# Key sums and attention products with 64 stationary columns, in steps of eight heads

## The chip, the cores and the metric

The kernel runs on one core of a Trainium2 chip. The time is the device time of one execution in microseconds; for the kernel before, three runs were timed. A profile of one execution shows when each engine worked: PE (TensorE: matmuls, with PEld the loads of the stationary operand), DVE (VectorE), ACT (ScalarE), POOL (GpSimd) and SP, which issues the transfers.

## The reference

Linear attention with random features, followed by a feed-forward block with a residual. Batch 8, 8 heads, 576 positions, head size 64, 128 features, model width 512, hidden width 2048, everything fp32:

```python
def phi(x):
    proj = np.einsum('bhsd,md->bhsm', x, omega)
    h = proj - np.sum(x * x, axis=-1, keepdims=True) / 2.0
    return np.exp(h - np.max(h, axis=-1, keepdims=True)) / np.sqrt(m)
q_p, k_p = phi(q * scale), phi(k * scale)
kv = np.einsum('bhsm,bhsd->bhmd', k_p, v)
z = np.sum(k_p, axis=2)
num = np.einsum('bhsm,bhmd->bhsd', q_p, kv)
den = np.einsum('bhsm,bhm->bhs', q_p, z)[..., None] + 1e-06
x = num / den                      # (b, h, s, d), then to (b, s, h*d)
xn = (x - mean(x)) / sqrt(var(x) + 1e-06) * g_ln
out = x + np.maximum(xn @ w_ch1, 0.0) @ w_ch2
```

## The kernel before

**Work and tiles.** The 8 x 576 = 4608 positions are nine MLP tiles of 512 (t) or 36 chunks of 128 (c). A batch has four and a half chunks: for the keys, each batch has four whole chunks, and the two halves that are left of a pair of batches share one mixed chunk; among the query chunks, four of the 36 lie in two batches.

- *Keys* (`gen_k`): the projection (L510, line numbers as in the profile) fills two PSUM banks, DVE takes the maximum (L442), ACT the exponential (L448). Then the **key sums** (`sums`, L480): per head, the 128 positions by 128 features of `kp` are the stationary operand, and the values with a column of ones (65 columns) are the moving one. That gives `kv` and `z` together. From batch 1 on each chunk's result goes to a bank of its own, and `keep` (L495) adds it into `kv` in SBUF.
- *Queries* (`gen_q2`, `features`): a projection in two matmuls (L582, L583), the maximum over features on POOL, subtraction on DVE, the exponential on ACT.
- *Products* (`gen_x`, L671): per head, 128 features by 128 positions are the stationary operand, `kv` with its 65 columns the moving one. DVE divides (L678, L680, L682) and frees the bank. Mean and variance (L698, L700) and the root (`gen_rs`) follow, then the normalising (L741), four transposes on PE (L755), a copy on ACT (L759) and a subtraction on DVE (L761), which leave the normalised input in two fp32r parts.
- *MLP* (`mm1`, `mm2`): three matmuls for each product of tiles, from the high and low parts (L782 to L784, L815 to L817), moving 512 columns each. The hidden parts come from ACT (L793) and DVE (L795).

An fp32 matmul of a row of the program is two matmuls in the profile; those of the MLP are one.

**PSUM.** Of eight banks, once the MLP has begun, four hold its output, two its hidden products, and two (`b_at`) are for all of attention: projections, key sums, products and transposes.

**What sets the order.** `Plan` writes the whole program's order ahead of time, by a list of estimated costs: a part asks for a place (`get`), waits for a result (`wait`) or takes an engine for an estimated time (`us`, `act`, `dve`), and among the parts that could start first the one with the lowest rank is taken. The MLP has the last rank (`Plan.FILL`), so it fills what the others leave of PE. Each engine then runs its instructions strictly in that order. Before the MLP begins (`mlp_on` is empty) `warm` fills PE with bf16 matmuls (L308) that compute nothing.

In the kernel before, the key sums and the products are parts of four heads each, and each takes one bank of `b_at` (for a mixed chunk of keys: two, one for each batch). Four heads are given 0.9 us of PE.

Of the kernel before, what the change touches and what calls it, by code (L numbers as in the profile page):

```python
# [190 lines left out]
def favor_ffn(ctx, tc, kT, kTr, vF, vR, qT, qD, omT, gT, w1, w2, out):  # L191
# [30 lines left out]
    def us(eng, t):  # L222
        return "run", {eng: t}
# [16 lines left out]
    def wait(*key):  # L240
        return "wait", key
# [13 lines left out]
    def bank(tag, n=512):  # L255
        return tile_of(tag, [P, 512], F32, ps)[:, 0:n]
# [12 lines left out]
    def at_now():  # L269
        return b_at if mlp_on else banks  # L270
# [67 lines left out]
    def gen_w(n, f):  # L338
# [81 lines left out]
    def gen_k(b, c, kraw, v, early, t_v, n_kp):  # L420
        rank = plan.cur.rank
        yield dma(2 * P * NP * P)
        nc.sync.dma_start(kraw, kT[b, c] if c < NFULL else kTr[b // 2])
        nc.sync.dma_start(v, vF[b, c] if c < NFULL else vR[b // 2])
        if c:
            yield wait("k", b, c - 1)
        t_kp = yield "get", n_kp
        t_mb = yield "get", n_mb
        late = t_kp, t_mb, t_v
        done(("k", b, c))  # L430
        kp = tile_of(late[0], [P, H, M])
        mb = tile_of(late[1], [P, H])
        yield wait("om")

        def values():
            yield us(DVE, 0.08)
            nc.vector.memset(v[:, :, D : D + 1], 1.0)
            done(("v", b, c))

        def side(s, t_b, pk):  # L440
            yield dve(4 * M)
            nc.vector.tensor_reduce(  # L442
                out=mb[:, 4 * s : 4 * s + 4], in_=pk, axis=AX.X, op=ALU.max, negate=True
            )
            yield act(M, 4, 0.142)
            for i in range(4):
                j = 4 * s + i
                nc.scalar.activation(  # L448
                    out=kp[:, j], in_=pk[:, i], func=AF.Exp, scale=1.0, bias=mb[:, j : j + 1]
                )  # L450
            free(t_b)
            done(("kp", b, c, s))

        def sums(s):
            yield wait("v", b, c)
            yield wait("kp", b, c, 0)
            yield wait("kp", b, c, 1)
            if c:
                yield wait("kvmm", b, c - 1, s)

            parts = [(b, slice(0, P))] if c < NFULL else [(b, slice(0, REM)), (b + 1, slice(REM, P))]
            t_b = []
            for n, _ in parts:
                if n or c == 0:
                    t_b.append((yield "get", at_now()))
                else:
                    t_b.append(pvs[s])
            if b == c == 0:
                pvs[s] = t_b[0]
                pvt[s] = bank(t_b[0])  # L470
            pv = [
                (bank(x) if n else pvt[s])[:, 0 : 4 * (D + 1)].rearrange("p (a b) -> p a b", b=D + 1)
                for x, (n, _) in zip(t_b, parts)
            ]
            yield us(PE, 0.9 if b else 1.13)
            for i in range(4):
                h = 4 * s + i
                for o, (n, r) in zip(pv, parts):

                    nc.tensor.matmul(  # L480
                        o[:, i], kp[r, slot(h)], v[r, h],
                        start=(n > 0 or c + i == 0), stop=(n > 0 or (c == NFULL and i == 3)),
                    )
                warm(i % 2)
            done(("kvmm", b, c, s))
            for x, o, (n, _) in zip(t_b, pv, parts):
                if n or c == NFULL:
                    plan.add(rank, keep(n, s, x, o))

        def keep(n, s, t_b, pv):  # L490
            o = kvs[n][1][:, 4 * s : 4 * s + 4]
            if n and (c if n == b else 0) or (n % 2 and c < NFULL):
                yield wait(*kv_key(n, c - 1), s)
                yield dve(4 * (D + 1))
                nc.vector.tensor_tensor(out=o, in0=pv, in1=o, op=ALU.add)  # L495
# [153 lines left out]
    def gen_x(c, t_st, st):  # L649
        blk, cols = c // 2, (c % 2) * P  # L650
        ends = sorted({0, P, *(b * S - c * P for b in range(B) if 0 < b * S - c * P < P)})
        parts = [(a, z, (c * P + a) // S) for a, z in zip(ends, ends[1:])]
        for j in range(2):
            for s in range(2):
                yield wait("phi", blk, j, s)
# [5 lines left out]
        o = 16 * (c % 2)  # L661
        rank = plan.cur.rank

        def half(s):
            t_b = yield "get", at_now()
            yield us(PE, 0.9 * len(parts) if mlp_on else 1.13)
            pn = bank(t_b)[:, 0 : 4 * (D + 1)].rearrange("p (a b) -> p a b", b=D + 1)
            for i in range(4):
                h = 4 * s + i
                for a, z, b in parts:  # L670
                    nc.tensor.matmul(  # L671
                        pn[a:z, i], phi(blk, h, slice(cols + a, cols + z)), kvs[b][1][:, h], start=True, stop=True
                    )
                warm(i % 2)
            done(("nummm", c, s))
            dn = st[:, o + 4 * s : o + 4 * s + 4]
            yield us(DVE, 0.13)
            nc.vector.tensor_scalar(out=dn, in0=pn[:, :, D], scalar1=EPS * M, scalar2=None, op0=ALU.add)  # L678
# [16 lines left out]
        yield wait("x", c, 0)  # L695
        bn, mv = st[:, o + 8 : o + 14], st[:, 32 + 2 * (c % 2) : 34 + 2 * (c % 2)]
        yield dve(DM)
        nc.vector.bn_stats(bn, x)  # L698
# [228 lines left out]
```

## Time and profile before

| | |
|---|---|
| Median of three runs | 1043.0 us (1042.22 to 1043.11) |
| Span of the profiled execution, first to last instruction | 1040.8 us |
| PE busy in the span | 1032.0 us, 99% |
| DVE, ACT, POOL busy | 498.3, 357.1 and 133.5 us |
| Granted TensorE clock | 1.000 |
| First MLP matmul | 49.07 us |

The profile gives no other time of its execution than the span; the median of the runs is 2.2 us above it. "Busy" counts an instruction from its start to its end, and matmuls overlap, so that a busy PE can still have room between starts. A row of the groups by line reads: line, engine, operation, written and read tiles, stationary shape (rows\*columns), moving shape, count, then the busy time in us and the mean ns of one, then the idle time of the engine just before and what ended it. A row of the order of time reads: start in us, length in us, engine, line, operation, tiles, shapes, count. A row of the waits reads: who waited, for whom, us in total, how often, the longest.

### The profile page before, as it was taken

The numbers are of one execution on the slowest core, as the hardware profiler recorded it, in microseconds if no ns is written. First come the engines' busy times: TensorE is split into PE (matmuls) and PEld (weight loads), VectorE is DVE, ScalarE is ACT, GpSimd is POOL, SyncE is SP. The second block draws the span as 40 slices with busy tenths as digits, with TensorE's granted clock in tenths as the row PEclk, the third lists the DMA queues.
The fourth block names the chain that finished last, engine by engine and source line by source line (L and its number), as shares of the span: only waits on it lengthen the run. The fifth ranks groups of instructions, "written<-read, shape, count | busy, mean of one in ns | idle before, by whom it ended". The sixth has DMA issues, their size and how long they took to land.

```text
span 1040.8 us, 14483 instructions
## 1 busy us (share of the span) xinstructions
PE 1032.0 (99%) x5778; PEld 863.4 (83%) x5778; DVE 498.3 (48%) x1045; ACT 357.1 (34%) x810; POOL 133.5 (13%) x80
## 2 busy tenths in 40 slices
PE   9999999999999999999999999999999999999998
PEld 7888888888887888888887888888878888888886
DVE  6999878366347521663147422751274134113112
ACT  7699746335334421253025421241133111102100
POOL 6000424014002300050002200140022000000000
PEclk9999999999999999999999999999999999999999
DMA  9564222121213100420032100200030010001001
GB/s 358 213 195 150 82 82 91 62 72 51 73 43 130 42 11 1 143 61 1 1 99 85 41 1 1 102 21 1 1 122 1 0 41 1 1 1 42 1 1 41
DMA packets 30308, 64.08 MB, mean 62 GB/s; under 512 B 3488, under 2 KB 3616, under 8 KB 30240
## 3 DMA queue, kind: packets, MB, share of 16 engines
q1 hardware_dynamic: 30240, 63.14, 17.9%
q8 instruction: 46, 0.75, 0.3%
q14 instruction: 22, 0.18, 0.1%
HBM read 53.69 MB, written 9.44 MB: 61 GB/s over the span
## 4 chain that ended last, share of the span: by engine, by line
PE 93%; DVE 4%; DMA 2%; SPq 1%; issue 1%; ACT 0%; ACTq 0%
PE b L815 13%; PE b L782 13%; PE b L784 12%; PE b L817 12%; PE b L816 12%; PE b L783 12%; PE b L480 5%; PE b L671 5%; PE b L510 3%; PE b L582 1%; PE b L583 1%; PE b L755 1%; DMA w<-w 1%; DVE x L826 1%; DMA w<-vF 0%
## 5 line engine op out<-in xcount | busy, mean ns | idle before, releaser
L795 DVE SCALAR_TENSOR_TENSOR hid<-b,hid 128x512 fp32r<-128x512 f32 x144 | 99.3, 689 | 382.5 <-ACT hid L793 381.9
L793 ACT ACTIVATE hid<-b 128x512 fp32r<-128x512 f32 x144 | 86.3, 599 | 445.8 <-PE b L784 445.4
L815 PE MATMUL b<-w,hid 128*128 128x512 f32 x576 | 231.6, 402 | 0.0
L782 PE MATMUL b<-xnT,w 128*128 128x512 f32 x576 | 230.4, 400 | 0.0
L817 PE MATMUL b<-w,hid 128*128 128x512 f32 x576 | 225.2, 391 | 0.0
L784 PE MATMUL b<-xnT,w 128*128 128x512 f32 x576 | 225.0, 391 | 0.1
L816 PE MATMUL b<-w,hid 128*128 128x512 f32 x576 | 224.9, 390 | 0.0
L783 PE MATMUL b<-xnT,w 128*128 128x512 f32 x576 | 224.5, 390 | 0.0
L604 POOL PARTITION_ALL_REDUCE wide<-wide x72 | 132.4, 1877 | 658.2 <-ACT st L713 268.3
L784 PEld LDWEIGHTS b<-xnT,w 128*128 128x128 f32 x576 | 108.2, 188 | 23.6 <-DVE xnT L761 0.5
L817 PEld LDWEIGHTS b<-w,hid 128*128 128x128 f32 x576 | 108.2, 188 | 23.0
L815 PEld LDWEIGHTS b<-w,hid 128*128 128x128 f32 x576 | 108.4, 188 | 22.6
L782 PEld LDWEIGHTS b<-xnT,w 128*128 128x128 f32 x576 | 108.4, 188 | 21.8
L783 PEld LDWEIGHTS b<-xnT,w 128*128 128x128 f32 x576 | 108.4, 188 | 20.6
L816 PEld LDWEIGHTS b<-w,hid 128*128 128x128 f32 x576 | 108.5, 188 | 20.3
L448 ACT ACTIVATE kp<-b,mb 128x128 f32<-128x128 f32 x272 | 75.3, 388 | 51.4 <-DVE mb L442 51.4
L671 PEld LDWEIGHTS b<-kv,wide 128*128 128x128 f32 (+1 forms) x640 | 67.2, 181 | 6.9 <-issue 2.8
L607 DVE TENSOR_TENSOR wide<-wide,wide 128x512 f32<-128x512 f32 x72 | 65.1, 909 | 13.3 <-POOL wide L604 12.8
L480 PEld LDWEIGHTS b<-v,kp 128*128 128x128 f32 (+1 forms) x576 | 64.2, 191 | 6.5 <-issue 1.6
L671 PE MATMUL b<-kv,wide 128*128 128x65 f32 (+1 forms) x640 | 66.8, 261 | 2.3 <-DVE st L678 1.2
L480 PE MATMUL b<-v,kp 128*128 128x65 f32 (+1 forms) x576 | 64.0, 272 | 0.0
L442 DVE TENSOR_REDUCE mb<-b 128x4 f32<-128x512 f32 x72 | 46.6, 681 | 30.9 <-PE b L510 30.8
(71 smaller groups left out, 800.0 us busy)
## 6 DMA issues: line engine op xcount, KB each, us to landing
w<-w SPq DMA_DIRECT2D x32, 512.0 KB, 8.9
wide<-qD SPq DMA_DIRECT2D x64, 256.0 KB, 2.7
out<-x SPq DMA_DIRECT2D x36, 256.0 KB, 2.0
v<-vF SPq DMA_DIRECT2D x28, 260.0 KB, 2.9
wide<-kT SPq DMA_DIRECT2D x28, 256.0 KB, 2.7
w<-vF SPq DMA_DIRECT2D x4, 260.0 KB, 4.8
v<-vR SPq DMA_DIRECT2D x4, 260.0 KB, 4.0
w<-kT SPq DMA_DIRECT2D x4, 256.0 KB, 4.8
```

The lines of the kernel that those rows point to most:

```text
L448: nc.scalar.activation(out=kp[:, j], in_=pk[:, i], func=AF.Exp, scale=1.0, bias=mb[:, j : j + 1])
L480: nc.tensor.matmul(o[:, i], kp[r, slot(h)], v[r, h], start=(n > 0 or c + i == 0), stop=(n > 0 or (c == NFULL and i == 3)),)
L604: nc.gpsimd.partition_all_reduce(mx, qc, P, bass_isa.ReduceOp.max)
L671: nc.tensor.matmul(pn[a:z, i], phi(blk, h, slice(cols + a, cols + z)), kvs[b][1][:, h], start=True, stop=True)
L782: nc.tensor.matmul(ph, w[:, 0, cs], xnT[:, 0, k], start=(k == 0), stop=False)
L783: nc.tensor.matmul(ph, w[:, 1, cs], xnT[:, 0, k], start=False, stop=False)
L784: nc.tensor.matmul(ph, w[:, 0, cs], xnT[:, 1, k], start=False, stop=(k == NK - 1))
L793: nc.scalar.activation(out=hl[:, 0], in_=ph, func=AF.Relu)
L795: nc.vector.scalar_tensor_tensor(out=hl[:, 1], in0=ph, scalar=0.0, in1=f32(hl[:, 0]), op0=ALU.max, op1=ALU.subtract)
L815: nc.tensor.matmul(accs[i], hl[:, 0, cs], w[:, 0], start=(f == 0), stop=False)
L816: nc.tensor.matmul(accs[i], hl[:, 0, cs], w[:, 1], start=False, stop=False)
L817: nc.tensor.matmul(accs[i], hl[:, 1, cs], w[:, 0], start=False, stop=(f == NF - 1))
```

## The change

Once the MLP has begun, a key sum or product of 128 stationary columns is written as two matmuls of 64 columns, each into its half of the PSUM partitions. The whole chunks' key sums (from batch 1 on) and all products become one part of eight heads, which asks for both banks of `b_at` at once and holds them until DVE is done with each. The mixed chunks' key sums stay at four heads, and their matmuls become 64 rows by 64 columns. The plan is told 0.46 us for each four heads and 0.3 us beside, where it had 0.9 for four heads. A mixed chunk of queries was already written in two pieces of 64 positions.

```diff
+    def column_tiles():
+        return [slice(0, P // 2), slice(P // 2, P)] if mlp_on else [slice(0, P)]
...
-        def sums(s):
+        def sums(heads):
...
-                    t_b.append((yield "get", at_now()))
...
+            new = [(s, n) for s in heads for n, _ in parts if n or c == 0]
+            t_b = dict(zip(new, (yield "get", at_now(), len(new)))) if new else {}
...
-            yield us(PE, 0.9 if b else 1.13)
-            for i in range(4):
-                h = 4 * s + i
-                for o, (n, r) in zip(pv, parts):
-
-                    nc.tensor.matmul(
-                        o[:, i], kp[r, slot(h)], v[r, h],
-                        start=(n > 0 or c + i == 0), stop=(n > 0 or (c == NFULL and i == 3)),
-                    )
-                warm(i % 2)
...
+            yield us(PE, (0.46 * len(heads) + 0.3) if b else 1.13)
+            for s in heads:
+                for i in range(4):
+                    h = 4 * s + i
+                    for m in column_tiles():
+                        for n, r in parts:
+                            nc.tensor.matmul(
+                                pv[s, n][m, i], kp[r, slot(h), m], v[r, h],
+                                start=(n > 0 or c + i == 0), stop=(n > 0 or (c == NFULL and i == 3)),
+                            )
+                    warm(i % 2)
+                done(("kvmm", b, c, s))
...
-        plan.add(rank, sums(0))
-        yield from sums(1)
-        yield wait("kvmm", b, c, 0)
+        if b and c < NFULL:
+            yield from sums((0, 1))
+        else:
+            plan.add(rank, sums((0,)))
+            yield from sums((1,))
+            yield wait("kvmm", b, c, 0)
...
+        halves = [(a, a + P // 2, (c * P + a) // S) for a in (0, P // 2)]
...
-        def half(s):
-            t_b = yield "get", at_now()
-            yield us(PE, 0.9 * len(parts) if mlp_on else 1.13)
...
+        def products(heads):
+            t_b = yield "get", at_now(), len(heads)
+            yield us(PE, (0.46 * len(heads) + 0.3) if mlp_on else 1.13 * len(heads))
...
+                    for a, z, b in halves if mlp_on else parts:
...
+            for s, pn, t in zip(heads, pns, t_b):
+                plan.add(rank, divided(s, pn, t))
...
-        plan.add(rank, half(0))
-        yield from half(1)
-        yield wait("nummm", c, 0)
+        for heads in [(0, 1)] if mlp_on else [(0,), (1,)]:
+            plan.add(rank, products(heads))
+        for s in range(2):
+            yield wait("nummm", c, s)
```

The program's new order, in three places. New line numbers of the same operations: L480 is now L483, L671 is L680, L510 is L514, L582 and L583 are L589 and L590, L755 is L770, L782 to L784 are L797 to L799, L815 to L817 are L830 to L832; on DVE, L495 is L499, L575 is L582, the division is L691 to L695, L741 is L756 and L761 is L776.

First, PE at two key sums of whole chunks in tile 2 (`b` is a PSUM bank, its number a use of it). Before:

```order
L480 MATMUL b_3036<-v_2848,kp_2934 128x65 x4
L480 MATMUL b_3045<-v_2848,kp_2934 128x65 x4
L815 MATMUL b_2057<-w_130_1376,hid_2986 128x512
L816 MATMUL b_2057<-w_130_1376,hid_2986 128x512
L817 MATMUL b_2057<-w_130_1376,hid_2986 128x512
L480 MATMUL b_3062<-v_2936,kp_2955 128x65 x4
L480 MATMUL b_3067<-v_2936,kp_2955 128x65 x4
```

Now:

```order
L483 MATMUL b_3289<-v_2966,kp_3056 64x65 x8
L483 MATMUL b_3290<-v_2966,kp_3056 64x65 x8
L797 MATMUL b_3291<-xnT_3208,w_00_368 128x512
L798 MATMUL b_3291<-xnT_3208,w_00_368 128x512
L799 MATMUL b_3291<-xnT_3208,w_00_368 128x512
L797 MATMUL b_3291<-xnT_3208,w_10_483 128x512
L798 MATMUL b_3291<-xnT_3208,w_10_483 128x512
L799 MATMUL b_3291<-xnT_3208,w_10_483 128x512
L483 MATMUL b_3320<-v_3058,kp_3090 64x65 x8
L483 MATMUL b_3321<-v_3058,kp_3090 64x65 x8
```

Sixteen rows of the program, 32 matmuls of the profile, stand where eight and 16 stood. Three MLP matmuls stood between halves of two chunks, six stand between whole steps. There are ten such pairs of key sums with six MLP matmuls between.

Second, PE at the end of tile 0, where tile 1's normalised chunks (`wide`) are transposed. Before, from the third chunk's transposes on:

```order
L755 MATMUL b_1911<-ident,wide_1868 128x128 x4
L815 MATMUL b_805<-w_140_1398,hid_1785 128x512
L816 MATMUL b_805<-w_140_1398,hid_1785 128x512
L817 MATMUL b_805<-w_140_1398,hid_1785 128x512
L755 MATMUL b_1922<-ident,wide_1871 128x128 x4
L815 MATMUL b_783<-w_150_1404,hid_1859 128x512
L816 MATMUL b_783<-w_150_1404,hid_1859 128x512
L817 MATMUL b_783<-w_150_1404,hid_1859 128x512
```

Three more such groups of three and a key sum of four heads follow, and then tile 1's first matmul (L782). Now, from behind the last products of chunk 7 (both its halves stand just ahead, and ahead of these the last MLP matmul of tile 0):

```order
L770 MATMUL b_1946<-ident,wide_1933 128x128 x4
L770 MATMUL b_1953<-ident,wide_1940 128x128 x4
L589 MATMUL b_1968<-wide_1844,om_hi 128x512
L590 MATMUL b_1968<-wide_1844,om_lo 128x512
L589 MATMUL b_1982<-wide_1853,om_hi 128x512
L590 MATMUL b_1982<-wide_1853,om_lo 128x512
L589 MATMUL b_1987<-wide_1928,om_hi 128x512
L590 MATMUL b_1987<-wide_1928,om_lo 128x512
L589 MATMUL b_2003<-wide_1937,om_hi 128x512
L590 MATMUL b_2003<-wide_1937,om_lo 128x512
L770 MATMUL b_2009<-ident,wide_1997 128x128 x4
L770 MATMUL b_2016<-ident,wide_1999 128x128 x4
```

The next row is tile 1's first matmul (L797). The four chunks' transposes now have no MLP matmul among or behind them, and the products of chunks 6 and 7 have three MLP matmuls between them.

Third, DVE at the same place, from behind the last division of tile 1's four chunks (`x_1717` is chunk 7, `st` its statistics, `xnT` the transposed input). Now:

```order
L713 BN_STATS st_1007<-x_1717 128x6
L715 BN_AGGR st_1007<-st_1007 128x2
L776 TENSOR_TENSOR xnT_1939<-b_1946,xnT_1939 128x4x128
L726 TENSOR_SCALAR st_1007<-st_1007 128x2
L582 TENSOR_TENSOR wide_1928<-wide_1905,wide_1928 64x512
L776 TENSOR_TENSOR xnT_1939<-b_1953,xnT_1939 128x4x128
L732 TENSOR_TENSOR st_1007<-st_1007 128x2
L582 TENSOR_TENSOR wide_1937<-wide_1931,wide_1937 64x512
L734 TENSOR_TENSOR st_1007<-st_1007 128x2
L736 TENSOR_SCALAR st_1007<-st_1007 128x2
L738 TENSOR_TENSOR st_1007<-st_1007 128x2
L756 TENSOR_SCALAR wide_1997<-x_1716,st_1007 128x512
```

The statistics, root and normalising of chunks 6 and 7 stand among the subtractions of chunks 4 and 5. Before, all statistics of the four chunks stood ahead of the first transposes.

More of the change, by code (lines that the diff above doesn't have):

```diff
@@ L458, in sums @@
             if c:
-                yield wait("kvmm", b, c - 1, s)
+                for s in heads:
+                    yield wait("kvmm", b, c - 1, s)
             parts = [(b, slice(0, P))] if c < NFULL else [(b, slice(0, REM)), (b + 1, slice(REM, P))]
-            t_b = []
-            for n, _ in parts:
-                if n or c == 0:
-                    t_b.append((yield "get", at_now()))
[L466 to L474, printed above, removed]
-            yield us(PE, 0.9 if b else 1.13)
-            for i in range(4):
-                h = 4 * s + i
-                for o, (n, r) in zip(pv, parts):
-                    nc.tensor.matmul(
-                        o[:, i], kp[r, slot(h)], v[r, h],
-                        start=(n > 0 or c + i == 0), stop=(n > 0 or (c == NFULL and i == 3)),
-                    )
-                warm(i % 2)
@@ L485, in sums @@
[L485 to L488, printed above, removed]
+            new = [(s, n) for s in heads for n, _ in parts if n or c == 0]
+            t_b = dict(zip(new, (yield "get", at_now(), len(new)))) if new else {}
+            for s in heads:
+                if b == c == 0:
+                    pvs[s] = t_b[s, 0]
+                    pvt[s] = bank(t_b[s, 0])
+                t_b.setdefault((s, 0), pvs.get(s))
@@ new lines, in sums @@
+            pv = {
+                (s, n): (bank(x) if n else pvt[s])[:, 0 : 4 * (D + 1)].rearrange("p (a b) -> p a b", b=D + 1)
+                for (s, n), x in t_b.items() if x
+            }
+            yield us(PE, (0.46 * len(heads) + 0.3) if b else 1.13)
+            for s in heads:
+                for i in range(4):
[8 more added lines that the diff above has]
+                done(("kvmm", b, c, s))
@@ L490, in keep @@
+            for s in heads:
+                for n, _ in parts:
+                    if n or c == NFULL:
+                        plan.add(rank, keep(n, s, t_b[s, n], pv[s, n]))
         def keep(n, s, t_b, pv):
@@ L662, in gen_x, with divided @@
         rank = plan.cur.rank
-        def half(s):
-            t_b = yield "get", at_now()
-            yield us(PE, 0.9 * len(parts) if mlp_on else 1.13)
[L667 to L675, printed above, removed]
+        def products(heads):
+            t_b = yield "get", at_now(), len(heads)
+            yield us(PE, (0.46 * len(heads) + 0.3) if mlp_on else 1.13 * len(heads))
+            pns = [bank(t)[:, 0 : 4 * (D + 1)].rearrange("p (a b) -> p a b", b=D + 1) for t in t_b]
+            for s, pn in zip(heads, pns):
+                for i in range(4):
+                    h = 4 * s + i
+                    for a, z, b in halves if mlp_on else parts:
+                        nc.tensor.matmul(
+                            pn[a:z, i], phi(blk, h, slice(cols + a, cols + z)), kvs[b][1][:, h], start=True, stop=True
+                        )
+                    warm(i % 2)
+                done(("nummm", c, s))
+            for s, pn, t in zip(heads, pns, t_b):
+                plan.add(rank, divided(s, pn, t))
+        def divided(s, pn, t_b):
             dn = st[:, o + 4 * s : o + 4 * s + 4]
@@ L689, in half @@
             done(("x", c, s))
-        plan.add(rank, half(0))
-        yield from half(1)
-        yield wait("nummm", c, 0)
+        for heads in [(0, 1)] if mlp_on else [(0,), (1,)]:
+            plan.add(rank, products(heads))
+        for s in range(2):
+            yield wait("nummm", c, s)
         done(("num", c))
-        yield wait("x", c, 0)
+        for s in range(2):
+            yield wait("x", c, s)
         bn, mv = st[:, o + 8 : o + 14], st[:, 32 + 2 * (c % 2) : 34 + 2 * (c % 2)]
```

## The prediction

> **What bounds the kernel now.** I read the page's totals first, then who waited for whom, then the groups by line and shape, and last the order of time around single steps.
>
> The totals:
>
> ```profile
> span 1040.8 us, 14483 instructions
> PE 1032.0 (99%) x5778; PEld 863.4 (83%) x5778; DVE 498.3 (48%) x1045; ACT 357.1 (34%) x810; POOL 133.5 (13%) x80
> PE 93%; DVE 4%; DMA 2%; SPq 1%; issue 1%; ACT 0%; ACTq 0%
> ```
>
> PE is busy for 99% of the span and is 93% of the chain that ended last; DVE is half empty. The waits of PE after the MLP has begun:
>
> ```profile
> PE b L671 <- DVE st L678: 1.2, 1, 1.2
> PE b L582 <- DVE st L678: 1.1, 1, 1.1
> PE b L671 <- DVE st L723: 1.0, 1, 1.0
> ```
>
> That is 3.3 us in all. So the time is the sum of what PE's instructions cost, plus a head and a tail: whatever an attention step saves on PE comes off the end, unless PE then waits. A busy share doesn't price a step, because matmuls overlap; the distance between starts does. Here is a step of eight heads with 128 stationary columns, between MLP matmuls:
>
> ```profile
> 137.58 0.40 PE L784 MATMUL b<-xnT,w 128*128 128x512 f32 x1
> 137.81 1.89 PE L671 MATMUL b<-kv,wide 128*128 128x65 f32 x16
> 139.51 0.47 PE L782 MATMUL b<-xnT,w 128*128 128x512 f32 x1
> 139.83 0.39 PE L783 MATMUL b<-xnT,w 128*128 128x512 f32 x1
> ```
>
> And here eight heads as 64 stationary columns, which the kernel already does for a chunk that lies in two batches:
>
> ```profile
> 763.92 0.40 PE L815 MATMUL b<-w,hid 128*128 128x512 f32 x1
> 764.16 0.39 PE L816 MATMUL b<-w,hid 128*128 128x512 f32 x1
> 764.38 0.40 PE L817 MATMUL b<-w,hid 128*128 128x512 f32 x1
> 764.71 1.15 PE L671 MATMUL b<-kv,wide 128*64 128x65 f32 x32
> 765.79 0.51 PE L815 MATMUL b<-w,hid 128*128 128x512 f32 x1
> 766.13 0.40 PE L816 MATMUL b<-w,hid 128*128 128x512 f32 x1
> ```
>
> An MLP matmul takes 0.23 us from start to start (763.92 to 764.38 is two). I take the time from the last MLP matmul ahead of a step to the second behind it, less two such distances: 139.83 - 137.58 - 0.46 = 1.79 us for the sixteen wide matmuls, 766.13 - 764.38 - 0.46 = 1.29 us for the thirty-two narrow ones. Narrow is cheaper by 0.50 us. Four heads alone:
>
> ```profile
> 131.14 0.39 PE L817 MATMUL b<-w,hid 128*128 128x512 f32 x1
> 131.46 0.69 PE L671 MATMUL b<-kv,wide 128*64 128x65 f32 x16
> 132.07 0.50 PE L582 MATMUL b<-wide,om_hi 128*128 128x512 f32 x1
> 132.41 0.39 PE L583 MATMUL b<-wide,om_lo 128*128 128x512 f32 x1
> ```
>
> 132.41 - 131.14 - 0.46 = 0.81 us, where half of the wide step is 0.90. So a narrow step has a fixed part (2 x 0.81 - 1.29 = 0.33 us) and 0.03 us for each matmul; with four heads it would win 0.09, with eight it wins 0.50. The two halves of this change need each other.
>
> **The change part by part.** How many steps there are:
>
> ```profile
> L671 PE MATMUL b<-kv,wide 128*128 128x65 f32 x512 | 62.0, 270 | 2.3 <-DVE st L678 1.2 <-DVE st L723 1.0
> L480 PE MATMUL b<-v,kp 128*128 128x65 f32 x448 | 54.5, 270 | 0.0
> L480 PE MATMUL b<-v,kp 64*128 64x65 f32 x128 | 9.5, 281 | 0.0
> L671 PE MATMUL b<-kv,wide 128*64 128x65 f32 x128 | 4.8, 225 | 0.0
> ```
>
> *Products.* 512 wide matmuls are 32 whole chunks of 16; four chunks belong to the first tile, before the MLP, and stay as they are. 28 x 0.50 = **-14.0 us**. *Key sums.* 448 are the 28 whole chunks of batches 1 to 7, and no row shows them narrow. Their operands have the products' sizes, so I take the products' price, 28 x 0.50 = **-14.0 us**.
>
> *Products of the four mixed chunks* are narrow already. One of them ran as two steps (131.46 and another), and joining saves 0.33 us. The two L671 waits above stand in mixed chunks, at the second half's bank; with both banks taken at once there is no second request: **-2.2 us**. The L582 wait of 1.1 I leave in.
>
> *Key sums of the mixed chunks* (64 rows of each of two batches) stay at four heads, 6 steps after the MLP has begun, and become 64 by 64:
>
> ```profile
> 206.41 0.40 PE L784 MATMUL b<-xnT,w 128*128 128x512 f32 x1
> 206.73 1.11 PE L480 MATMUL b<-v,kp 64*128 64x65 f32 x16
> 207.77 0.50 PE L782 MATMUL b<-xnT,w 128*128 128x512 f32 x1
> 208.11 0.40 PE L783 MATMUL b<-xnT,w 128*128 128x512 f32 x1
> ```
>
> Now 208.11 - 206.41 - 0.46 = 1.24 us. The trace has no 64 by 64 matmul. If all four quarters ran beside each other, its 32 matmuls would cost what 16 narrow ones do, 0.81; if only pairs did, what 32 do, 1.29. I take the middle, 1.05: **-1.1 us** (-2.6 to +0.3).
>
> Sum of what goes: 14.0 + 14.0 + 0.3 + 2.2 + 1.1 = 31.6 us.
>
> *What comes.* The order of PE's instructions shows one place where PE will have nothing to do. Tile 1's first MLP matmul needs four transposed chunks. Now their transposes stand among the last MLP matmuls of tile 0, the last one here:
>
> ```profile
> 162.51 0.60 PE L755 MATMUL b<-ident,wide 128*128 128x128 f32 x4
> 166.62 0.40 PE L782 MATMUL b<-xnT,w 128*128 128x512 f32 x1
> ```
>
> 4.1 us filled with MLP work and a key sum hide the copy and the subtraction. In the changed order the products need both banks free together and come later: those of chunk 7 stand *behind* the last MLP matmul of tile 0, and behind them only two pairs of transposes and eight query matmuls, and then tile 1. So the whole chain from chunk 7's products (division, statistics, root, normalising, transposing, copy) stands open. The nearest row is the same chain before the MLP begins, from the last product of tile 0 to its first MLP matmul:
>
> ```profile
> 37.72 0.56 PE L671 MATMUL b<-kv,wide 128*128 128x65 f32 x4
> 49.07 0.48 PE L782 MATMUL b<-xnT,w 128*128 128x512 f32 x1
> ```
>
> 49.07 - 38.28 = 10.8 us, with DVE also on other work, as it will be here. Off this go PE's own instructions in between: sixteen transposes and eight query matmuls at 0.23. The transposes' row stands below with DVE's for the same chain; by it and the row at 162.51 they follow each other at (0.60 - 0.27) / 3 = 0.11 us. Together 3.6 us, which leaves 7.2.
>
> ```profile
> L755 PE MATMUL b<-ident,wide 128*128 128x128 f32 x144 | 20.2, 273 | 0.4 <-DVE wide L741 0.4
> ...
> L682 DVE TENSOR_TENSOR x<-b,st 128x256 f32<-128x256 f32 x72 | 30.0, 421 | 1.1
> L698 DVE BATCH_NORM_STATS2 st<-x 128x6 f32<-128x512 f32 x36 | 24.8, 689 | 0.6
> L741 DVE TENSOR_SCALAR wide<-x,st 128x512 f32<-128x512 f32 x36 | 18.6, 539 | 0.1
> L761 DVE TENSOR_TENSOR xnT<-b,xnT 128x512 fp32r<-128x512 f32 x36 | 23.9, 685 | 7.7 <-ACT xnT L759 7.7
> L680 DVE RECIPROCAL st<-st 128x4 f32<-128x4 f32 x72 | 12.2, 173 | 1.0
> L678 DVE TENSOR_SCALAR st<-b 128x4 f32<-128x4 f32 x72 | 10.9, 154 | 11.8 <-PE b L671 11.1
> L495 DVE TENSOR_TENSOR kv<-b,kv 128x260 f32<-128x260 f32 x56 | 23.8, 427 | 49.8 <-PE b L480 49.7
> ```
>
> One chunk's division of both halves is 2 x (0.154 + 0.173 + 0.421) = 1.5 us. Chunk 7's products follow chunk 6's after three MLP matmuls (0.68 us) and need the banks that this division frees: about 0.8 us more. I take **+8 us**. From below: the bare chain of one chunk, 1.5 + 0.69 + 2 x 0.54 + 0.69 and an estimated 1.5 for the small operations (eight of L678's size, with hand-overs) is 5.5, less 3.6: 2 us. From above: 10.8 with no cover but the transposes, 10 us.
>
> *Two banks at once, elsewhere.* The steps now stand close at ten places where key sums follow key sums after six MLP matmuls (6 x 0.23 = 1.4 us), and four where products do. Behind a key sum the two additions into the sums must be done, 2 x 0.427 = 0.85 us and the hand-over: covered, unless DVE is in something else of 0.69. Behind products stand nine or more (2.0 us) against 1.5. I take **+1 us** for all of it, 0 to 5; if cover failed at every one of some 30 close places by half a microsecond, 15. *Head:* the same work in a slightly other order, with eight more filler matmuls on PE: **+0.5 us**, 0 to 1.4. Loads are reordered among themselves a little; DMA is 2% of the chain.
>
> Sum against the profiled span: 1040.8 - 31.6 + 8 + 1 + 0.5 = 1018.7 us. The median of the runs is 1043.0, 2.2 above the span, so I forecast **1021 us**. The likeliest case's own range is 1014 to 1027.
>
> [...]
>
> **Rivals.**
>
> 1. *The stall at tile 1 is hidden or short* (up to 3 us), because DVE is less loaded there than at the head. For it: DVE is 48% busy. Against: the order leaves PE nothing. 1043.0 - 31.6 + 1.5 + 2 = 1015 us.
> 2. *Both banks are missed often.* PE meets a step whose banks DVE hasn't freed, half a microsecond at some 30 close places: 15 us in place of 1, 1035 us. For it: the three waits above are of just this kind. Against: there are three in a thousand microseconds.
> 3. *Narrow key sums don't run in pairs* (slower). If each narrow matmul takes half a wide one's 1.79 / 16 = 0.112 us, a step is 32 x 0.056 + 0.33 = 2.1 us: with both kinds so, 56 x 0.33 = 18 us lost instead of 28 saved. 1043.0 + 18 - 2.5 + 9.5 = 1068 us. A step breaks even at (1.79 - 0.33) / 32 = 0.046 us per matmul, and with the other terms the case decides from 0.042 on. For it: no row shows a narrow key sum, nor two such steps close together. Against: the row at 764.71. [...]
> 4. *PE's time goes but the end stays*, since something else sets it, 1043 us. Against: PE's share of the chain; nothing else has more than 4%.
>
> **How the numbers follow.** The forecast has 0.62, rival 1 0.15, rival 2 0.17, rivals 3 and 4 0.03 each. The range 1011 to 1031 takes in the forecast with its bounds, rival 1 and the milder half of rival 2. A measurement of this kernel can tell about 0.2% (2 us) from no change. Faster: the first three, 0.94; the same 0.02; slower 0.04.
>
> **What would show it.** In the changed profile: key sums and products as groups of 32 of shape 128*64, 1.29 us each by the same subtraction; wrong if a step is over 1.5. Key sums of mixed chunks between 0.81 and 1.29. Around 155 to 170 us PE with idle time before the transposes, the query matmuls and tile 1's first L797, ended by DVE or ACT, 8 us together; if PE has no gap there, rival 1. Elsewhere waits of PE for L499 or L695 of some 1 us in all; over 10 is rival 2. PE's last matmul some 22 us earlier than before.

## The result, and the profile after

The changed kernel takes **1023.7 us** (median of four runs, 1023.02 to 1024.31) against 1043.05 for the kernel before: a ratio of 0.9814, with a 95% interval of 0.98 to 0.9828. The forecast was 1021 us, 1011 to 1031. The time is inside the range; two terms of the sum are outside their own bounds, the gap before tile 1 and the head, and the experiments are mostly about the gap.

The page's totals of the changed kernel (L483 is now the key sums, L680 the products, L770 the transposes, L776 the subtraction behind them, L797 to L799 and L830 to L832 the MLP):

```profile
span 1022.3 us, 16484 instructions
PE 1009.1 (99%) x6778; PEld 818.1 (80%) x6778; DVE 500.2 (49%) x1057; ACT 351.2 (34%) x798; POOL 135.3 (13%) x80
PE 93%; DVE 3%; DMA 2%; SPq 0%; issue 0%; ACT 0%; DVEq 0%
```

PE is still what sets the end: 1000 matmuls more, and 23 us less of busy time. The groups by line and shape show the change itself, all key sums and products with 64 columns:

```profile
L680 PE MATMUL b<-kv,wide 128*64 128x65 f32 x1024 | 37.1, 224 | 0.5 <-DVE st L732 0.4 <-DVE x L695 0.2
L483 PE MATMUL b<-v,kp 128*64 128x65 f32 x896 | 32.5, 224 | 0.9 <-DVE v L440 0.9
L483 PE MATMUL b<-v,kp 64*64 64x65 f32 x192 | 4.2, 224 | 0.0
```

The price of one step, in the order of time: first a key sum of eight heads, then a mixed chunk's key sum of four heads as 64 by 64.

```profile
150.12 0.39 PE L832 MATMUL b<-w,hid 128*128 128x512 f32 x1
150.44 1.15 PE L483 MATMUL b<-v,kp 128*64 128x65 f32 x32
151.52 0.50 PE L830 MATMUL b<-w,hid 128*128 128x512 f32 x1
151.86 0.40 PE L831 MATMUL b<-w,hid 128*128 128x512 f32 x1
...
220.17 0.39 PE L832 MATMUL b<-w,hid 128*128 128x512 f32 x1
220.49 0.70 PE L483 MATMUL b<-v,kp 64*64 64x65 f32 x32
221.11 0.50 PE L797 MATMUL b<-xnT,w 128*128 128x512 f32 x1
221.45 0.39 PE L798 MATMUL b<-xnT,w 128*128 128x512 f32 x1
```

151.86 - 150.12 - 0.46 = 1.28 us for eight heads of key sums, which the trace of before could not show, and 221.45 - 220.17 - 0.46 = 0.82 us for the 64 by 64.

Where the time came back is at the border from tile 0 to tile 1. PE's waits there, from the view of waits, and the order of time:

```profile
PE b L770 <- DVE st L693: 3.4, 1, 3.4
PE b L770 <- DVE wide L756: 1.7, 2, 1.5
PE b L483 <- DVE v L440: 0.9, 1, 0.9
```

```profile
158.79 0.40 PE L832 MATMUL b<-w,hid 128*128 128x512 f32 x1
159.34 0.69 PE L680 MATMUL b<-kv,wide 128*64 128x65 f32 x16 [0.15 <-DVE x L695]
160.39 0.69 PE L680 MATMUL b<-kv,wide 128*64 128x65 f32 x16 [0.37 <-DVE st L732]
164.47 1.94 PE L770 MATMUL b<-ident,wide 128*128 128x128 f32 x8 [3.39 <-DVE st L693]
...
173.04 1.94 PE L770 MATMUL b<-ident,wide 128*128 128x128 f32 x8 [1.45 <-DVE wide L756]
175.81 0.79 PE L797 MATMUL b<-xnT,w 128*128 128x512 f32 x1 [0.83 <-ACT xnT L774]
...
180.73 0.40 PE L797 MATMUL b<-xnT,w 128*128 128x512 f32 x1
```

From the last MLP matmul of tile 0 to the first of tile 1 it is 175.81 - 158.79 = 17.0 us. PE's own work in between is worth about 5.1: one MLP matmul 0.23, the products 1.28, sixteen transposes at 0.11, eight query matmuls at 0.23. So 11.9 us are lost up to there. PE is idle for 7.0 of them by the order of time; the rest is work that takes longer. The transposes also show something else: eight take 1.94 us, where a group of eight lasted 1.04 in the trace of before. The windows of time say why (columns: from:to, length, busy time of PE, PEld, DVE, ACT and POOL, granted clock, DMA share, GB/s):

```profile
163.44:175.81 12.37, 8.22 (x24) 5.30 (x25) 10.73 (x22) 6.29 (x14) 5.36 (x4) 0.50 0.15 48
175.81:180.50 4.69, 4.69 (x22) 3.42 (x23) 3.94 (x7) 2.35 (x5) 1.91 (x2) 0.50 0.68 225
```

With the gap the granted clock fell to half, and it stayed there until 180.50, 4.7 us after tile 1 had begun. The first stretch of tile 1, 175.81 to 180.73, takes 4.92 us; the same stretch takes 2.76 at full clock (it is shown in the third experiment). The busy share of PE hides all of this: in the second of these windows PE is busy for 4.69 us of 4.69, at half clock.

### The profile page after: what moved, and what is told of

It reads as the page before. It is cut to its first block, busy times and chain, and to the rows that moved or that the text cites. A ratio compares the mean times of both kernels' runs of the same rounds, so it can differ in the third digit from the quotient of the medians.

```text
span 1022.3 us, 16484 instructions
## 1 busy us (share of the span) xinstructions
PE 1009.1 (99%) x6778; PEld 818.1 (80%) x6778; DVE 500.2 (49%) x1057; ACT 351.2 (34%) x798; POOL 135.3 (13%) x80
## 4 chain that ended last, share of the span: by engine, by line
PE 93%; DVE 3%; DMA 2%; SPq 0%; issue 0%; ACT 0%; DVEq 0%
PE b L830 14%; PE b L797 14%; PE b L799 13%; PE b L798 13%; PE b L831 13%; PE b L832 13%; PE b L514 3%; PE b L483 3%; PE b L680 3%; DMA w<-w 2%; PE b L770 1%; PE b L589 1%; PE b L590 1%; DMA w<-vF 1%; DVE x L841 1%
## 5 line engine op out<-in xcount | busy, mean ns | idle before, releaser
L808 ACT ACTIVATE hid<-b 128x512 fp32r<-128x512 f32 x144 | 86.2, 598 | 434.6 <-PE b L799 433.7
L830 PE MATMUL b<-w,hid 128*128 128x512 f32 x576 | 232.3, 403 | 0.0
L797 PE MATMUL b<-xnT,w 128*128 128x512 f32 x576 | 229.7, 399 | 0.8 <-ACT xnT L774 0.8
L799 PE MATMUL b<-xnT,w 128*128 128x512 f32 x576 | 224.8, 390 | 0.1
L832 PE MATMUL b<-w,hid 128*128 128x512 f32 x576 | 224.8, 390 | 0.0
L797 PEld LDWEIGHTS b<-xnT,w 128*128 128x128 f32 x576 | 108.3, 188 | 25.9 <-ACT xnT L774 1.2
L830 PEld LDWEIGHTS b<-w,hid 128*128 128x128 f32 x576 | 108.1, 188 | 25.0
L799 PEld LDWEIGHTS b<-xnT,w 128*128 128x128 f32 x576 | 108.4, 188 | 23.8 <-DVE xnT L776 0.9
L832 PEld LDWEIGHTS b<-w,hid 128*128 128x128 f32 x576 | 108.1, 188 | 23.2
L614 DVE TENSOR_TENSOR wide<-wide,wide 128x512 f32<-128x512 f32 x72 | 62.8, 875 | 6.0 <-POOL wide L611 5.5
L617 ACT ACTIVATE wide<-wide 128x512 f32<-128x512 f32 x72 | 45.5, 636 | 42.4 <-DVE wide L614 40.1
L582 DVE TENSOR_TENSOR wide<-wide,wide 64x512 fp32r<-64x512 f32 x64 | 51.5, 806 | 10.1 <-ACT wide L580 8.3
L230 ACT COPY wide<-b 128x512 f32<-128x512 f32 x58 | 33.3, 592 | 54.1 <-PE b L590 49.8
L680 PEld LDWEIGHTS b<-kv,wide 128*64 128x64 f32 (+1 forms) x1088 | 40.7, 140 | 12.1 <-issue 8.1
```

What stands on the lines that cost most here:

```text
L614: nc.vector.tensor_tensor(out=qc, in0=qc, in1=mx, op=ALU.subtract)
L680: nc.tensor.matmul(pn[a:z, i], phi(blk, h, slice(cols + a, cols + z)), kvs[b][1][:, h], start=True, stop=True)
L797: nc.tensor.matmul(ph, w[:, 0, cs], xnT[:, 0, k], start=(k == 0), stop=False)
L799: nc.tensor.matmul(ph, w[:, 0, cs], xnT[:, 1, k], start=False, stop=(k == NK - 1))
L808: nc.scalar.activation(out=hl[:, 0], in_=ph, func=AF.Relu)
L830: nc.tensor.matmul(accs[i], hl[:, 0, cs], w[:, 0], start=(f == 0), stop=False)
```

## The experiments

The theory after the result: narrow matmuls gain what was forecast; asking for both banks at once moves tile 1's inputs behind all of tile 0's work, and the gap costs some 14 us, part of it through the clock and part through slow work on DVE. Each experiment undoes or isolates one of these. All times are medians, ratios against the kernel before.

### Narrow matmuls in the order of before

The kernel before, with its steps of four heads and its order, where only the matmuls are made narrow:

```diff
...
-                for o, (n, r) in zip(pv, parts):
-                    nc.tensor.matmul(o[:, i], kp[r, slot(h)], v[r, h], ...)
+                for m in column_tiles():
+                    for o, (n, r) in zip(pv, parts):
+                        nc.tensor.matmul(o[m, i], kp[r, slot(h), m], v[r, h], ...)
...
-                for a, z, b in parts:
+                for a, z, b in halves if mlp_on else parts:
```

> The kernel before with only its matmuls made narrow (64 stationary columns, mixed key sums 64 by 64); steps stay at four heads, the plan's costs and so the order on every engine stay those of the kernel before. Theory (the price of a step is 0.33 us for a run of narrow matmuls and 0.03 for each; neighbouring halves share the 0.33): 13 double key sums and 22 double products save 0.51 each, about 36 single halves 0.09 each, a triple and the mixed products 2.2, mixed key sums 2.5 together; about 26 us saved, no stall at tile 1, the three waits of before remain: 1017 us (1015 to 1020), less than the change itself takes. Rival (a narrow step arrives before its banks or inputs are ready when the order was made for slower steps): over half of the saving comes back as waits of PE, 1028 or more.

Measured: **1019.3 us** (1019.12 to 1019.49), 0.9772 (0.9757 to 0.9787). Half of the change alone is quicker than the whole of it. Why four heads win so much stands in its order of time; here two steps of four heads, which the order of before put next to each other, and then in its waits (L675 products, L585 a query's matmul):

```profile
282.43 0.39 PE L821 MATMUL b<-w,hid 128*128 128x512 f32 x1
282.75 1.15 PE L483 MATMUL b<-v,kp 128*64 128x65 f32 x32
...
284.17 0.39 PE L820 MATMUL b<-w,hid 128*128 128x512 f32 x1
```

```profile
PE b L585 <- DVE st L682: 1.3, 1, 1.3
PE b L675 <- DVE st L682: 1.2, 1, 1.2
PE b L675 <- DVE st L727: 1.2, 1, 1.2
```

284.17 - 282.43 - 0.46 = 1.28 us: two neighbouring steps of four cost what one step of eight does, since the fixed part of 0.33 us is paid once for a run of narrow matmuls, whoever issued them. Counted over the trace, 29 of the 56 key-sum steps and 52 of the 64 product steps have such a neighbour with no wait between. That leaves 79 runs where the change has 60: 19 x 0.33 = 6.3 us, an estimate; the distances, summed over both traces without the waits, differ by 7.0. So joining the heads is worth 6 to 7 us and the three waits (3.7), some 10 us in all, and costs the gap.

### Eight heads at once, wide

The other half alone: the changed kernel with 128 columns, and the plan told 0.9 us per four heads as before.

```diff
     def column_tiles():
-        return [slice(0, P // 2), slice(P // 2, P)] if mlp_on else [slice(0, P)]
+        return [slice(0, P)]
...
-            yield us(PE, (0.46 * len(heads) + 0.3) if b else 1.13)
+            yield us(PE, 0.9 * len(heads) if b else 1.13)
...
-                    for a, z, b in halves if mlp_on else parts:
+                    for a, z, b in parts:
```

> The change with its matmuls left wide (128 stationary columns) and the plan told 0.9 us for four heads; steps of eight heads that take both banks at once. Theory (the stall at tile 1 comes from asking for both banks at once, not from narrow matmuls): steps cost 1.79 us as before, PE has idle time of 8 us or more before tile 1 and its clock falls there; 1043 + 14 to 18 - 2.2 for the waits of before that go, so 1055 to 1060 us. Rival (the stall comes from narrow steps, the banks cost nothing): 1041 to 1044 us and no idle time of PE before tile 1.

Measured: **1058.5 us** (1056.79 to 1058.65), 1.0143 (1.0126 to 1.0159): slower than before, as the theory had it. Its waits at the same border:

```profile
PE b L770 <- DVE xnT L776: 2.7, 2, 2.0
PE b L589 <- ACT kp L451: 2.0, 1, 2.0
```

The two rows hold three of the six waits from 165 to 187 us, which come to 7.3 us. A gap comes without narrow matmuls, so it is a matter of the two banks and the order that goes with them.

### The clock alone

In the changed kernel, 40 bf16 matmuls that compute nothing (L313) are put into the gap, without telling the plan, so that every engine keeps its order:

```diff
+    def fill(n):
+        fil = bank(b_h[1])[:, 0 : 2 * P]
+        for _ in range(n):
+            nc.tensor.matmul(fil, spin[:, 0:P], spin, start=True, stop=True)
...
+            if c == 2 * TC - 1:
+                fill(20)
...
+        if t == 1 and i % 2:
+            fill(10)
```

> The change, with forty bf16 matmuls that compute nothing added on PE in the stall before tile 1 (twenty behind chunk 7's products, ten behind each second pair of transposes) without telling the plan, so that the order of everything else is the change's own; the earlier filled kernel had moved other steps too. Theory (the chain there is set by DVE and ACT, and the halved clock costs only what PE does behind it, 2.2 us by the distances between starts from tile 1's first matmul to the clock's return): granted clock 1.00, tile 1 starts at the same time after tile 0's end as in the change, within half a microsecond, and 2 us are saved: 1021.6 us (1021 to 1022.4). Rival (slow transposes and query matmuls lengthen the chain as well): 4 to 5 us saved, 1019 us.

Measured: **1021.9 us** (1021.55 to 1023.32), 0.9795 (0.9779 to 0.9812). In its order of time (L839 to L841 and L806 to L808 are the MLP):

```profile
159.83 0.40 PE L841 MATMUL b<-w,hid 128*128 128x512 f32 x1
177.21 0.48 PE L806 MATMUL b<-xnT,w 128*128 128x512 f32 x1
179.97 0.39 PE L806 MATMUL b<-xnT,w 128*128 128x512 f32 x1
```

The gap is as long as ever, 177.21 - 159.83 = 17.4 us, though most of it now lies at full clock. Behind it the same stretch takes 179.97 - 177.21 = 2.76 us in place of 4.92. So the half clock costs 2.2 us in tile 1. The median moved by 1.8.

That it costs nothing inside the gap is not shown, since the fillers held tile 1 up themselves. Its first matmul waits for ACT's second cast, here first in the change and then with fillers:

```profile
175.18 0.58 ACT L774 CAST xnT<-b 128x512 fp32r<-128x512 f32 x1
175.64 0.58 ACT L783 CAST xnT<-b 128x512 fp32r<-128x512 f32 x1
```

In the change the cast ends at 175.76, 17.0 us after tile 0's last matmul began, and tile 1 starts at once. With fillers it ends at 176.22, after 16.4 us, and PE is in its last ten fillers until tile 1 starts 1.0 us later. So the input was there 0.6 us earlier, although the second transposes still ran at half clock (1.81 us for eight).

An earlier version of this told the plan of the fillers:

```diff
+                    if t == 1:
+                        yield wait("nummm", 2 * TC - 1, 1)
+                        t_b = yield "get", (b_h[1],)
+                        fil = bank(t_b)[:, 0 : 2 * P]
+                        while ("xnT", 1, TC - 1) not in plan.made:
+                            yield us(PE, 0.15)
+                            nc.tensor.matmul(fil, spin[:, 0:P], spin, start=True, stop=True)
+                        free(t_b)
```

> The change, with small bf16 matmuls that compute nothing put into PE's stall before tile 1 (from behind chunk 7's products until tile 1's input is there). Theory (part of the loss there is PE's halved clock, 17 us long in the profile of the change): the granted clock stays at 1.00 throughout and transposes, query matmuls and the key projection there take full-speed lengths; 4 to 5 us saved, 1019 us (1017.5 to 1020.5). Rival (everything there waits for DVE and ACT, so the clock costs only what lies behind the stall): 1 to 2 us saved, 1022 us.

Measured: **1022.7 us** (1022.5 to 1023.13), 0.9805 (0.979 to 0.982). The theory's 1019 failed, but the plan had also moved other steps (one query step went ahead of tile 1, and tile 2 got a wait), so it decides little. Together they win 1 to 2 us, not the 4.7 that the expectation gave the clock; the first paid 1.0 us for its own last fillers, so this isn't the clock's whole price.

### No gap: the first tiles in fours

The changed kernel, but the products of chunks 4 to 7 (tile 1) and the key sums of batch 1 in steps of four heads, each asking for one bank:

```diff
-        if b and c < NFULL:
+        if b > 1 and c < NFULL:
...
-        for heads in [(0, 1)] if mlp_on else [(0,), (1,)]:
+        for heads in [(0, 1)] if c >= 8 else [(0,), (1,)]:
```

> The change, but tile 1's products (chunks 4 to 7) and batch 1's key sums in steps of four heads, each with one bank; narrow everywhere, eight heads everywhere else. In the order tile 1's transposes then stand among MLP matmuls again. Theory (the 14 us that the change loses around tile 1 come from both banks being asked for at once there): 14 us saved, less 8 steps more at 0.33 us and about 1 us of waits at the ends of tiles 0 and 1: 1013 us (1011.5 to 1016). Rival (the lateness moves to another tile's start, or DVE is simply behind): 1018 or more.

Measured: **1014.5 us** (1013.61 to 1014.74), 0.9724 (0.971 to 0.9739), with a granted clock of 1.000. Undoing the joining at four chunks and four key sums wins 9.3 us over the change. The gap is shown to be the cost of asking for two banks where tile 1 depends on it.

### Both together

The same, with batch 2's key sums in fours too, the plan told 0.76 us for four heads of products, 0.9 for four of key sums and 1.22 for eight, and the first tile's products planned by the code of before:

```diff
-            yield us(PE, (0.46 * len(heads) + 0.3) if b else 1.13)
+            yield us(PE, (1.22 if len(heads) > 1 else 0.9) if b else 1.13)
...
-        if b and c < NFULL:
+        if (b > 2) and c < NFULL:
...
-        for heads in [(0, 1)] if mlp_on else [(0,), (1,)]:
-            plan.add(rank, products(heads))
+        if c >= 8:
+            plan.add(rank, products((0, 1)))
+        else:
+            plan.add(rank, half(0))
+            yield from half(1)
```

> A version meant to be better than both: narrow matmuls everywhere; key sums of batches 1 and 2 and products of chunks 4 to 7 in steps of four heads with one bank (the plan is told 0.9 and 0.76 us for them), eight heads with both banks behind that; the head before the MLP planned as in the kernel before. In its order tile 1's and tile 2's transposes stand among MLP matmuls. Theory (the change loses about 14 us at tile 1 and 1.7 at the head, nothing else): 16 us less than the change, plus 12 steps more at up to 0.33 us: 1011.5 us (1010 to 1013), and a first MLP matmul at 49.1 us. Rival (each rearrangement only moves the wait to another place): 1014 or more, no better than the run with halves in tile 1 alone.

Measured: **1010.8 us** (1010.58 to 1011.03), 0.969 (0.9676 to 0.9704), the quickest of all. Its profiled span is 1008.8 us; the waits of PE above 0.1 us once the MLP has begun:

```profile
PE b L589 <- ACT kp L451: 0.3, 1, 0.3
PE b L787 <- DVE wide L773: 0.3, 1, 0.3
PE b L483 <- DVE xnT L793: 0.2, 1, 0.2
```

What is left of PE's waits is 0.8 us. The first MLP matmul starts at 49.40 us here, at 50.76 in the change. How much each of the bundled edits gives was not separated.

### VectorE's small operations and POOL

In the change's gap VectorE's operations of the root for chunks 6 and 7 (L734, L736, L738, 128 by 2 elements) are slow, while POOL reduces the next queries' features:

```profile
162.65 0.16 DVE L738 TENSOR_TENSOR st<-st 128x2 f32<-128x2 f32 x1
...
169.24 0.88 DVE L734 TENSOR_TENSOR st<-st 128x2 f32<-128x2 f32 x1
170.16 0.72 DVE L736 TENSOR_SCALAR st<-st 128x2 f32<-128x2 f32 x1
170.91 0.98 DVE L738 TENSOR_TENSOR st<-st 128x2 f32<-128x2 f32 x1
```

```profile
168.96 3.66 POOL L611 PARTITION_ALL_REDUCE wide<-wide  x2 [29.36 <-ACT wide L230]
```

The first row is the same operation for the chunks before, with POOL idle. A first try told the plan to put that reduction later:

```diff
+        if blk == T // QB * 2:
+            yield wait("xnT", 1, TC - 1)
         yield us(POOL, 1.9)
```

> The change, with the maxima over features on POOL for the four query pieces that are projected inside the stall held back until tile 1's input is complete; the order of DVE's operations from chunk 7's division to the normalising of chunks 6 and 7 is the change's own. Theory (DVE's small operations of the root, 0.72 to 0.98 us each there in place of 0.16, and the normalising, are slowed by POOL's work at the same time): these operations take 0.15 to 0.17 us and 0.54 each, tile 1's first matmul starts 14.6 us behind tile 0's last in place of 17.0, and the time is 1021.4 us (1020.5 to 1022.3). Rival (they wait for one another or for ACT, and POOL has no part in it): lengths and start as in the change, 1023 to 1024.5 us.

Measured: 1024.5 us (1022.46 to 1025.07), 0.9827 (0.9811 to 0.9844). Inconclusive: such a wait only moves places in each engine's list, and POOL, whose list it left alone, began as soon as its data were there: its two reductions (L613) run from 167.37 us for 3.66 us, and the three operations take 0.88, 0.72 and 0.98 us again.

The second try makes POOL wait by the data. Ahead of that reduction it reduces one column of the last thing that VectorE writes for tile 1:

```diff
...
             yield wait("xnT", 1, TC - 1)
+            if (j, s) == (0, 0):
+                nc.gpsimd.partition_all_reduce(
+                    hold, f32(xnTs[1][1][:, 1, 0, T - 1 : T]), P, bass_isa.ReduceOp.max
+                )
```

> In the run before this one (pool_later) the plan's wait moved nothing: POOL's all-reduce of the next queries' features still ran from 167.4 us, and VectorE's three root operations of chunk 7 (L734, L736, L738 of the change) still took 0.88, 0.72 and 0.98 us, the first normalisation behind them 1.35. Here POOL is made to wait by the data: ahead of the first of these all-reduces it reduces one column of chunk 7's transposed low part, which VectorE writes last of all before tile 1 begins. Nothing is left out; one all-reduce of 128x1 is added. Theory (POOL working at the same time is what slows VectorE's small operations): with POOL idle until tile 1 begins, the three take about 0.16 us each and the normalising 1.0, about 2.4 us less; tile 1's first matmul starts 14.2 to 14.9 us after tile 0's last one (16.6 in pool_later, 17.0 in the change), and the time is about 1021.4 us (1020.5 to 1022). Rival (they are slow for another reason that falls on the same moment, such as the transfers or ScalarE's copies): the three stay at 0.7 to 1.0 us with POOL idle, the distance stays at 16.4 to 17.2 us, and the time is 1023 to 1024.5 us.

Measured: **1021.1 us** (1020.49 to 1022.9), 0.9795 (0.9779 to 0.9812). The same three operations (here L741, L743, L745), POOL, and PE's last MLP matmul of tile 0 and first of tile 1:

```profile
168.39 0.16 DVE L741 TENSOR_TENSOR st<-st 128x2 f32<-128x2 f32 x1
168.58 0.17 DVE L743 TENSOR_SCALAR st<-st 128x2 f32<-128x2 f32 x1
168.79 0.16 DVE L745 TENSOR_TENSOR st<-st 128x2 f32<-128x2 f32 x1
```

```profile
174.48 0.85 POOL L614 PARTITION_ALL_REDUCE hold<-xnT  x1 [35.28 <-DVE xnT L783]
```

```profile
158.40 0.40 PE L839 MATMUL b<-w,hid 128*128 128x512 f32 x1
173.28 0.50 PE L804 MATMUL b<-xnT,w 128*128 128x512 f32 x1 [0.95 <-ACT xnT L781]
```

With POOL idle the three are back at 0.16 to 0.17 us, though the clock of PE was at half here too. The distance is 173.28 - 158.40 = 14.9 us in place of 17.0 in the change and 16.6 in the try before, and the time is 3.4 us under that try, 2.6 under the change; the four runs of each spread over some 2.5 us, so that these two figures are rough. The theory holds: it is POOL's reduction that slows them. What it won is more than their own time: the clock was back at 171.94, before tile 1 began, and tile 1's first eight matmuls take 2.67 us from start to start, where they take 3.84 at half clock in the try before. So 1.7 us lie in the distance and 1.2 behind it.

## Why the prediction was right, and where it was not

By its own steps, in us. "Measured" is the same subtraction of distances, summed over all steps of a kind in both traces.

| Term | forecast | measured |
|---|---|---|
| Products, with the joining and the L671 waits | -14.0 - 0.3 - 2.2 = -16.5 | -17.1 |
| Whole key sums | -14.0 | -14.4 |
| Mixed key sums | -1.1 (-2.6 to +0.3) | -2.5 |
| The L582 wait | 0, left in | -1.2 |
| Gap before tile 1, with the half clock behind it | +8 (2 to 10) | +14.1 |
| Waits for two banks elsewhere | +1 (0 to 5) | +0.9 |
| Head | +0.5 (0 to 1.4) | +1.7 |
| Sum on the span | -22.1 | -18.5 (span: -18.5) |

The measured sum is 3.6 us short of the forecast; the time is only 2.7 off, because the median stands 1.4 us above the profiled span and not 2.2. That it came so near is partly luck: the gap and the head cost 7.3 us more than forecast, and the first four rows, two of them mis-sized, gave 3.6 more.

**Right: the price of a narrow step.** 1.29 us was taken from a mixed chunk's products and carried over to all products and to key sums, of which no row existed; both came out at 1.28. Rival 3 (narrow key sums don't pair) fell with that.

**Right: the place of the gap and what ends it.** The waits stand where the prediction put them, before the transposes, the query matmuls and tile 1's first matmul, ended by DVE and ACT. Their 7.0 us are even near the 8 that the prediction looked for as a sign, but idle time is not what the gap costs: work at half clock comes on top. Rival 1 (the gap is hidden) fell. Rival 2 (both banks missed often) fell: one wait of 0.9 us elsewhere. Its row names L440, which sets the column of ones; but the first half of the same step had already read the same values, and straight ahead of the second half, at 304.59, DVE ended a subtraction that reads a bank (L776), late behind three others. So it was most likely the one bank that came late. Rival 4 (the end stays) fell with the time.

**Wrong: the size of the gap.** The step that failed is the analogy with the start of the kernel, 10.8 us less PE's own 3.6, with "no cover but the transposes" as the upper bound. Measured are 11.9 us up to tile 1's first matmul and 2.2 behind it, 14.1 in place of 8. The 0.8 for the banks was right: from the end of tile 0's last share, 158.79 + 0.23, to the end of chunk 7's products at 161.08 it is 2.1 us, and the products' own price is 1.28. The chain behind them took 175.81 - 161.08 = 14.7 us and not 10.8, 3.9 more, and for the 2.2 behind it the sum had no term. What the runs name:

- *The clock*, 2.2 us behind the gap (4.92 against 2.76). At the start of the kernel before, fillers run and the clock is full (PE busy for 10.35 us of the 10.79 from 38.28 to 49.07, at 1.00). This gap on PE had a price after its end, and no row of before showed one. Inside the gap it may have cost 0.6 us more, by the cast in the run with fillers.
- *POOL*. In the change the three operations and the normalising behind them end 2.2 us later than with POOL held back, of which PE's distance takes 1.7 (16.6 to 14.9, same order); the rest goes into PE's own query matmuls, which are then last. This one is shown by experiment. At the start of the kernel before, POOL does nothing in that window (busy for 0.00 us from 38.28 to 49.07).
- *DVE's queue*. Between chunk 6's and chunk 7's divisions DVE's list has two query subtractions (0.69 each) and chunk 6's statistics (0.69). Chunk 7's division began at 162.82, 1.7 us after its products had ended at 161.08. But the start of the kernel has such a delay too. The last division's first row, there and in the change:

```profile
39.51 0.13 DVE L678 TENSOR_SCALAR st<-b 128x4 f32<-128x4 f32 x1
163.41 0.13 DVE L691 TENSOR_SCALAR st<-b 128x4 f32<-128x4 f32 x1
```

That is 1.2 us behind the last product (38.28) and 2.3 behind it (161.08), so some 1.1 us of it is new. This is read from the traces and was not tested by itself.

Of the 3.9 us in the chain, 1.7 are shown to be POOL's; the clock's 0.6 and the queue's 1.1 are readings, and half a microsecond stays open. The two chains also differ in DVE's other work, so this is no full account.

**Wrong: "The two halves of this change need each other."** Four heads alone were priced at 0.81, against 0.90 wide, as if each step stood alone. But the very row that priced the wide step (137.81, sixteen matmuls) is two steps of four heads that stand next to each other in the kernel before. The narrow half alone gives 1019.3 us, two thirds of the 35 us that PE could save, without any gap.

**Mis-sized, and in favour.** The mixed key sums: the price of the case that all four quarters run beside each other came out, 0.82 against 0.81. The L582 wait went, which was left in. **The head** took 1.7 where 1.4 was the bound. One trace gives its size only roughly: in the seven traces with the change's head the first MLP matmul starts at 49.65 to 51.79 us, in the three with the head of before (narrow matmuls in the order of before 49.44, the first tile's products planned by the old code 49.40) at 49.07 to 49.44. So it is the new order of the head, not the narrow matmuls, which start behind it; what in that order it is stays open.

## What to carry to other kernels

Price a step by the distance between starts, and a *run* of like steps by one fixed part (0.33 us here): before joining two steps, see whether they already stand next to each other. Where a step takes all buffers of a kind at once, look first at the place with the shortest slack behind it (here the last products ahead of a tile's border), and let it take them one by one there only: that alone was worth 9 us over the change. Price a gap on PE with the half-clocked stretch behind it (4.92 us in place of 2.76 here), and see what else the waiting chain meets in that window, here POOL above all (0.72 to 0.98 us in place of 0.16 for each of three operations).

## What the runs showed of the hardware

**Half clock for whole multiples of 3.41 us.** At the gap the granted clock was at half for 17.07 us (change), 23.89 (eight heads wide), 13.65 (POOL later), 6.83 (POOL held) and 3.41 (fillers): five, seven, four, two and one times 3.41. In these five traces it came back at the end of the first such stretch that PE filled without a gap, as these windows of the change and of the kernel with POOL held show:

```profile
173.68:177.09 3.41, 2.58 (x10) 1.69 (x8) 2.57 (x5) 2.92 (x6) 2.98 (x2) 0.50 0.30 76
177.09:180.50 3.41, 3.41 (x20) 2.63 (x20) 2.66 (x5) 1.07 (x3) 0.63 (x1) 0.50 0.63 232
```

```profile
165.11:168.52 3.41, 2.26 (x6) 1.30 (x5) 3.25 (x9) 2.52 (x7) 0.00 (x0) 0.50 0.32 82
168.52:171.94 3.42, 3.42 (x11) 2.16 (x11) 1.45 (x5) 2.06 (x4) 0.00 (x0) 0.50 0.00 0
```

In the wide kernel the clock stayed at half behind a stretch with 3.26 us of PE's work (166.32 to 169.73), and came back behind the first full one (186.80 to 190.21). With POOL held it was back early, before tile 1 had begun: the query matmuls and transposes filled one stretch. In the run with fillers it fell at 173.78 after a stretch in which PE was still busy for a quarter, and went back up at 177.19:

```profile
170.36:173.78 3.42, 0.89 (x4) 0.48 (x5) 3.24 (x5) 1.13 (x3) 2.84 (x2) 1.00 0.00 0
```

In that stretch PE waited for 2.4 us in one piece. In these five traces the clock fell behind such stretches with 0.69 to 1.03 us of PE's work (0.69 in the change, 1.03 with POOL held), and stayed full behind one with 1.89 (158.28 to 161.70, POOL held); between the two these runs don't say. Nor is this all: the mean granted clock of the profiled execution with fillers is 0.996, where 3.41 us at half would leave 0.998, which its three other runs show. Where the rest was lost is not shown.

**VectorE's small operations while POOL reduces.** 0.16 us became 0.72 to 0.98. With POOL held back they took 0.16 to 0.17. They were slowed, not stopped until POOL was done: the first of the three ran from 169.24 to 170.12, between the start of the first reduction (168.96) and its end (about 170.79, half of the two's 3.66, as the profile times POOL), so it did not wait for that end.

**64 by 64.** 32 matmuls of 64 rows by 64 columns in four quarters cost 0.82 us, as much as 16 of 128 by 64 (0.81, in the kernel before): if the fixed 0.33 us is the same, 0.015 us each beyond it.
